# Value products over all 128 rows, conversions placed freely, reciprocal tile double and value tile single

## Chip, core and metric

The kernel runs on one NeuronCore of a Trainium2 chip, alone. The core has five engines that run side by side, each through its own list of instructions in a fixed order: TensorE (PE; its weight loads are shown apart, as PEld), VectorE (DVE), ScalarE (ACT), GpSimd (POOL) and SyncE (SP), whose list here is the queue that issues all transfers. The metric is the time on the device in microseconds; lower is better.

## What is computed

A block-causal attention over 4 batches, 8 heads, 576 positions and 64 channels is followed by two feed-forward layers, each with an inner width of 2048 over 2304 tokens of 512 channels. The weights of the layers come as 64-bit numbers.

```python
scores = scale * np.matmul(q, k.transpose(0, 1, 3, 2))
mask = block_i >= block_j                      # blocks of 64 positions
scores = np.where(mask, scores, -1000000000.0)
attn = np.exp(scores - np.max(scores, axis=-1, keepdims=True))
attn = attn / (np.sum(attn, axis=-1, keepdims=True) + 1e-09)
x = np.matmul(attn, v)                         # then (tokens, 512)
h = x @ w_in;  x = (h / (1 + np.exp(-h))) @ w_out
h = x @ w_in2; out = (h / (1 + np.exp(-1.702 * h))) @ w_out2
```

## The kernel before

**Pairs.** The attention works on 16 pairs of heads. Both heads of a pair fill the 128 rows. For each of nine blocks of 64 queries, `s_mm` forms the scores of both heads with a block-diagonal tile of the queries (`bd`) as the loaded operand and the keys as the streaming one. Every number is split into a rounded part and a residue (`qh`, `ql`, `kh`, `kl`, two halves of `va`, `pt0` and `pt1`), and three products take the place of one. `s_max` (L425, DVE) takes row maxima, `s_exp` (L435, ACT) exponentials with row sums, `t_mm` (L474, PE) transposes the probabilities in tiles of 128x128, `t_hi` (ACT, or DVE once) and `t_lo` (L492, DVE) split them into `pt0` and `pt1`.

**Value products.** `o_mm` multiplies values with transposed probabilities, head by head, in two halves of the query blocks. The loaded operand is 128 keys of the split values (`va`), the streaming one the probabilities of the query blocks that see these keys. The first half has four products (256 and 128 columns, for `pt0` and for `pt1`), the second half ten: 320, 320, 320, 192 and 64 columns, twice. 576 keys are four and a half tiles of 128, so the product of 64 columns has only 64 keys, and the kernel gives it 64 rows (L509). There are 32 blocks of ten, with 64 such products. The values are padded with zeros to 640 keys in memory (`layout_v`), and the last 64 columns of every probability tile of even index are set to zero once at the start (L595).

**Normalising.** `o_copy` moves the results to the tiles `e0` and `e1`, `x_shift` moves parts of them across the rows by transfers, and `x_add` adds (POOL). Reciprocals of the row sums (`r_inv`) go by way of a small tile and device memory (`r_mm`, `r_copy`, `r_put`) and come back spread over the rows as the tile `rb` (`r_get`, L465); `x_norm` (L545, POOL) multiplies. `rb` had one buffer. `v`, the value tile that `v_hi` (L326) and `v_lo` (L390) on POOL split into `va`, had two.

**Weights.** A weight piece of 128x512 arrives as 64-bit numbers in `raw` (two buffers, 512 KB, L232), and becomes single precision in six instructions: `w_scale` (L239, ACT), `w_bits` (L248, L250, DVE), `w_rest` (L260, L262, DVE) and `w_sum` (L270, POOL). Eight pieces are converted in the attention part; `w_part` enters one for every second pair, half of it in each of two rounds. The others follow in the feed-forward part.

**What sets the order.** Nothing is issued where it is written. `Flow.add` collects every operation with an assumed duration and what it reads and writes; `Flow.run` then plays them through: the engine that can start first takes, of its operations that are ready, the one with the lowest `at`. `at` comes from the table `plan`, whose rounds are 12.6 us (`TAU`) apart, pair after pair, in units of the planner's own clock. The argument `early` holds an operation back to a given planner time even when all it needs is there. `w_part` sets it to its own place plus 6 us (`T0`). The outcome is one fixed list per engine; on the chip an engine waits at each entry until its inputs and its buffer are free, and everything behind it on that engine waits too.

The feed-forward part has two layers in three phases each. A step forms one tile of the inner width (L667 to L669, 12 products), applies the activation (L682 to L687) and multiplies into four accumulators (L694 to L696, 12 products); the tokens go through in chunks of up to 512 (`xc`, L646 and L648).

Of the kernel before, what the change touches and what calls it, by code (L numbers as in the profile page):

```python
# [26 lines left out]
class Flow:  # L27
# [8 lines left out]
        self.wrote = {}  # L36
        self.read = {}

    def add(self, eng, us, fn, reads=(), writes=(), at=0.0, lag=0.0, size=0, after=(), name="", sb=False, early=0.0):
        op = Op()  # L40
        op.eng, op.us, op.fn, op.at, op.lag, op.size, op.name = eng, us, fn, at, lag, size, name
        op.outs, op.ready, op.end, op.idx, op.sb = [], early, 0.0, len(self.ops), sb
        deps = {id(x): x for x in after}
        for k in reads:
            w = self.wrote.get(k)
            if w is not None:
                deps[id(w)] = w
            self.read.setdefault(k, []).append(op)
        for k in writes:
            w = self.wrote.get(k)  # L50
            if w is not None:
                deps[id(w)] = w
            for x in self.read.get(k, ()):
                if x is not op:
                    deps[id(x)] = x
            self.wrote[k] = op
            self.read[k] = []
        op.left = len(deps)
        for x in deps.values():
            x.outs.append(op)  # L60
        self.ops.append(op)
        return op
# [47 lines left out]
def mm(n):  # L110
    return max(0.11, n / 2400 + 0.0135)
# [18 lines left out]
def block_causal_attention_two_ffn(  # L130
# [9 lines left out]
    nc = tc.nc  # L140
    PSUM = bass.MemoryType.PSUM

    NP, P, S = qT.shape
    BLK = 64
    NB = S // BLK
    NKT = vP.shape[2] // P
# [12 lines left out]
    NA = 4  # L159
    NWARM = 12  # L160
    TAU = 12.6
    T0 = 6.0
    LEAD = 12
    BEFORE = 1e4

    flow = Flow()
    add = flow.add
# [15 lines left out]
    def T(pool, shape, dt, name):  # L183
        if name not in tiles:
            tiles[name] = pools[pool].tile(shape, dt, tag=name, name=name)
        return tiles[name]

    bank = {i: T("psum", [P, 512], F32, f"bank{i}") for i in (0, 1, 4, 5, 6, 7)}
    sb = T("psum", [P, 2, 512], F32, "sb")
# [8 lines left out]
    def xkeys(m, c0, n):  # L198
        return [("xy", m, i) for i in range(c0 // H, (c0 + n - 1) // H + 1)]
# [25 lines left out]
    def w_load(op, n, i):  # L225
        l, f = divmod(n, NF)
        c = slice(i * DM, (i + 1) * DM)
        k = piece(n, i)
        if not WIDE:
            op("sp", 0.4, lambda: nc.sync.dma_start(out=wf_(k), in_=ws_[l][f][:, c]), (), [("wf", k % NWF)], size=P * DM * 4)  # L230
            return
        op("sp", 0.4, lambda: nc.sync.dma_start(  # L232
            out=raw_(k).rearrange("p d b -> p (d b)"), in_=ws_[l][f][:, c].bitcast(I32)), (), [("raw", k % 2)],
            size=P * DM * 8)
# [37 lines left out]
    def w_split(n, i, at):  # L272
        k = piece(n, i)
        kw, kh, kl = ("wf", k % NWF), ("ws", n % NS, i, 0), ("ws", n % NS, i, 1)
        add("act", 0.53, lambda: nc.scalar.copy(slot(n, i)[:, 0, :], wf_(k)), [kw], [kh], at, after=slot_after(n))  # L275
        add("pool", 1.28, lambda: nc.gpsimd.tensor_sub(slot(n, i)[:, 1, :], wf_(k), f32(slot(n, i)[:, 0, :])),  # L276
            [kw, kh], [kl], at, after=slot_after(n))
# [9 lines left out]

    ends = {"a1": [], "a2": [], "a3": []}
    clock = [0.0]
    early = [0.0]  # L290

    def op(eng, us, fn, reads=(), writes=(), lag=0.0, size=0, sb=False):
        x = add(eng, us, fn, reads, writes, clock[0] - BEFORE, lag=lag, size=size, name="att", sb=sb, early=early[0])
        for y in ends:
            ends[y].append(x)
        return x
# [13 lines left out]
    def a1(p, n):  # L310
        return T("a1", [P, S], F32 if n in "qk" else F32R, n + (str(p % 2) if n in ("kh", "kl") else ""))

    def ka1(p, n):
        return (n, p % 2 if n in ("kh", "kl") else 0)

    def a3(p, n, shape=None, dt=F32):
        return T("a3", shape or [P, S], dt, f"{n}_{p % 2}")

    def pt(p, i):
        return T("a2" if p % 2 == 0 else "a3", [P, nat, P], F32R, f"pt{i}_{p % 2}")  # L320
# [14 lines left out]
    def take(what, key):  # L335
        if what == "s":
            held[key] = S_BANK[key[2]]
        else:
            turn[what] += 1
            held[key] = ring[what][turn[what] % len(ring[what])]  # L340
        return held[key]

    def src(p, n):
        if p == 0 and n in "qk":
            return a3(0, {"q": "e0", "k": "e1"}[n]), ("e", 0, "qk".index(n))
        if n == "v":
            return a3(p, "v", [P, NKT * 2 * BLK]), ("v", p % 2)
        return a1(p, n), ka1(p, n)

    def load(p, n):  # L350
        t, k = src(p, n)
        d = {"q": qT, "k": kT, "v": vP}[n]
        op("sp", 0.4, lambda: nc.sync.dma_start(out=t, in_=d[p]), (), [k], size=P * d.shape[2] * 4)

    def q_hi(p, eng):
        (q, k), t = src(p, "q"), a1(p, "qh")
        op("act", act(S), lambda: nc.scalar.mul(t, q, BLK ** -0.5), [k], [ka1(p, "qh")])
# [4 lines left out]
    def q_lo(p):  # L362
        (q, k), t, hi = src(p, "q"), a1(p, "ql"), a1(p, "qh")
        op("dve", 0.67, lambda: q_sub(t, q, hi), [k, ka1(p, "qh")], [ka1(p, "ql")], sb=True)
# [16 lines left out]
    def va_(p):  # L381
        return a3(p, "va", [P, NKT * 2, 2, BLK], F32R)
# [71 lines left out]
    def rd_(p):  # L454
        return T("drp", [2, NB, BLK], F32, f"rd{p % 2}")
# [3 lines left out]
        op("sp", 0.4, lambda: nc.sync.dma_start(out=rd_(p).rearrange("h j q -> j h q"), in_=rt), [("rt", 0)], [("rd", p % 2)])  # L459

    def r_get(p):
        rb = a3(0, "rb")
        for h, r in enumerate((A, B)):
            s = rd_(p)[h:h + 1].rearrange("h j q -> h (j q)").to_broadcast([BLK, S])
            op("sp", 0.65, lambda r=r, s=s: nc.sync.dma_start(out=rb[r], in_=s), [("rd", p % 2)], [("rb", 0, h)],  # L465
               size=P * S * 2)

    def t_mm(p, g):
# [26 lines left out]
    def o_mm(p, h, half):  # L495
        j0, j1 = halves[half]
        n = (j1 - j0) * BLK
        b = take("o", ("o", p, h, half))
        o = bank[b]
        va = va_(p)  # L500
        seq = [(i, kt) for i in (0, 1) for kt in range(NKT) if 2 * kt < j1]
        fs = {fidx[kt, j] for _, kt in seq for j in range(max(j0, 2 * kt), j1)}
        gs = [g for g, x in enumerate(groups) if fs & set(x)]

        def mms():
            for a, (i, kt) in enumerate(seq):
                js = max(j0, 2 * kt)
                f = fidx[kt, js]
                r = slice(0, P if 2 * kt + 1 < NB else BLK)  # L509
                w = va[r, 2 * kt + h, :, :].rearrange("p a b -> p (a b)")  # L510
                x = pt(p, i)[r, f:f + j1 - js, h * BLK:(h + 1) * BLK]
                nc.tensor.matmul(o[:, (js - j0) * BLK:n], w, x, start=(a == 0), stop=(a == len(seq) - 1))  # L512

        us = sum(mm((j1 - max(j0, 2 * kt)) * BLK) * 1.05 for i, kt in seq)
        op("pe", us, mms, [("pt", p % 2, g, i) for g in gs for i in range(2)] + [("va", p % 2, 0), ("va", p % 2, 1)], [("B", b)], lag=0.2)
# [25 lines left out]

    def x_norm(p):
        b, hp = divmod(p, PPB)
        x, rb = a3(p, "x"), a3(0, "rb")
        op("pool", 1.45, lambda: nc.gpsimd.tensor_mul(xy[:, hp, b * S:(b + 1) * S], x, rb),  # L545
           [("x", p % 2, 0), ("x", p % 2, 1), ("rb", 0, 0), ("rb", 0, 1)], xkeys(hp, b * S, S))

    def w_part(p, stage):
        n = divmod((p + 1) // 2, 2)
        if p < 1 or n[0] >= NA or (stage < 2) != (p % 2 == 1):  # L550
            return
        early[0] = clock[0] + T0
        (w_scale, w_bits, w_rest, w_sum)[stage](op, *n)
        if stage == 2 and n != (NA - 1, 1):
            w_load(op, n[0] + n[1], 1 - n[1])
        early[0] = 0.0

    plan = [
        (0, s_mm, 3), (1, s_exp, 4), (0, s_max, 3), (2, o_mm, 0, 0), (1, t_mm, 2), (1, t_hi, 0, "act"),
# [10 lines left out]
        (0, s_exp, 5), (0, s_mm, 1), (1, t_mm, 5), (1, v_lo, "pool"), (1, t_mm, 1), (1, r_put),  # L570
        (0, w_part, 3), (0, s_max, 1), (0, s_mm, 4), (1, t_hi, 5, "dve"), (2, o_copy, 1, 1, "act"),
        (1, t_lo, 5), (0, s_exp, 1), (1, t_hi, 1, "act"), (2, r_get), (0, s_max, 4), (0, t_mm, 0),
        (1, t_lo, 1),
    ]
# [230 lines left out]
```

## Time and profile before

| | us |
|---|---|
| median of three runs | 1046.88 (1041.76 to 1050.94) |
| the profiled execution, its own time | 1043.87 |
| its span from the first to the last instruction | 1041.8 |
| PE busy | 1007.7 (97%) |
| DVE busy | 698.9 (67%) |
| ACT busy | 485.4 (47%) |
| POOL busy | 326.4 (31%) |

A busy share is the time in which an engine had an instruction in progress. Matmuls are pipelined: the next one starts before the one before it ends, and a busy TensorE is not one at its peak. How far matmuls really follow each other is read from the distance between their starts. The page's chain of work goes back from the last instruction, at each step to what released it; 80% of it is PE and 13% DVE. The idle time in a row is that of its engine just before the instruction, with what ended it.

### The profile page before, as it was taken

The page shows a single profiled execution, that of the slowest core. Times are in us where ns is not written, and L with a number is a line of the kernel's source. Part 1 is how long each engine was busy: PE and PEld are TensorE (multiplying, and loading weights), DVE is VectorE, ACT ScalarE, POOL GpSimd, SP SyncE. Part 2 cuts the span into 40 slices and gives each one's busy share as a digit, 9 for nine tenths or more (in the row PEclk, how much of TensorE's full clock was granted, in tenths as well). Part 3 has the DMA queues.
Part 4 walks back from the last instruction along what each step waited for, and adds up shares of the span by engine and source line. Part 5 has one row for each costly group of instructions (what it writes and reads, how often), then busy time and mean ns, then how long its engine had stood idle before and what let it go on. Part 6 is the DMA issues. An engine that isn't in the chain of part 4 may idle for free.

```text
span 1041.8 us, 14408 instructions
## 1 busy us (share of the span) xinstructions
PE 1007.7 (97%) x5196; PEld 854.1 (82%) x5196; DVE 698.9 (67%) x1144; ACT 485.4 (47%) x1055; POOL 326.4 (31%) x238
## 2 busy tenths in 40 slices
PE   7899999988999999999999999999999999999998
PEld 5788878776888898888988888888888888888887
DVE  6689987778989769954798348962359444454333
ACT  5677777675545355432543235442345332343221
POOL 6557665658544245210342006310016000000000
PEclk8999999999999999999999999999999999999999
DMA  6777867733234413542244111321112222112222
GB/s 180 177 182 169 207 162 178 192 84 93 72 117 156 137 66 127 176 142 81 81 142 133 50 41 57 106 102 41 41 54 89 81 81 81 62 61 81 81 82 81
DMA packets 84616, 112.67 MB, mean 108 GB/s; under 512 B 41920, under 2 KB 46528, under 8 KB 84544
## 3 DMA queue, kind: packets, MB, share of 16 engines
q1 hardware_dynamic: 84544, 111.74, 35.9%
q8 instruction: 41, 0.67, 0.3%
q14 instruction: 31, 0.25, 0.1%
HBM read 72.12 MB, written 23.67 MB: 92 GB/s over the span
## 4 chain that ended last, share of the span: by engine, by line
PE 80%; DVE 13%; ACT 3%; issue 2%; DMA 1%; POOL 0%; DVEq 0%; SPq 0%; ACTq 0%; POOLq 0%
PE bank L668 11%; PE bank L667 11%; PE bank L669 11%; PE sb L694 6%; PE sb L696 6%; PE sb L695 6%; PE bank L694 6%; PE bank L696 6%; PE bank L695 6%; PE bank L512 5%; PE bank L474 4%; DVE xc L648 2%; DVE mx L425 1%; DVE wf L250 1%; DVE pt L492 1%
## 5 line engine op out<-in xcount | busy, mean ns | idle before, releaser
L684 DVE SCALAR_TENSOR_TENSOR th<-th,bank 128x512 f32<-128x512 f32 (+1 forms) x160 | 100.9, 630 | 211.3 <-ACT th L682 211.0
L667 PE MATMUL bank<-xc,ws 128*128 128x512 f32 (+1 forms) x640 | 236.0, 369 | 0.0
L668 PE MATMUL bank<-xc,ws 128*128 128x512 f32 (+1 forms) x640 | 235.9, 369 | 0.0
L669 PE MATMUL bank<-xc,ws 128*128 128x512 f32 (+1 forms) x640 | 235.7, 368 | 0.0
L682 ACT ACTIVATE th<-bank 128x512 f32<-128x512 f32 (+1 forms) x160 | 88.6, 554 | 301.8 <-PE bank L669 295.9
L276 POOL TENSOR_TENSOR ws<-wf,ws 128x512 fp32r<-128x512 f32 x64 | 93.9, 1481 | 237.2 <-ACT ws L275 237.2
L686 ACT CAST g<-th 128x512 fp32r<-128x512 f32 (+1 forms) x160 | 92.5, 578 | 118.4 <-DVE th L684 118.3
L687 DVE TENSOR_TENSOR g<-th,g 128x512 fp32r<-128x512 f32 (+1 forms) x160 | 111.6, 698 | 45.3 <-ACT g L686 44.3
L270 POOL TENSOR_TENSOR wf<-wf,wt 128x512 f32<-128x512 f32 x64 | 91.2, 1425 | 160.4 <-DVE wt L262 160.4
L669 PEld LDWEIGHTS bank<-xc,ws 128*128 128x128 f32 x640 | 120.7, 189 | 20.4 <-DVE xc L648 0.2
L667 PEld LDWEIGHTS bank<-xc,ws 128*128 128x128 f32 x640 | 120.7, 189 | 20.1
L668 PEld LDWEIGHTS bank<-xc,ws 128*128 128x128 f32 x640 | 120.7, 189 | 19.8
L694 PE MATMUL sb<-g,ws 128*128 128x512 f32 (+1 forms) x320 | 118.4, 370 | 4.4 <-ACT g L686 2.6
L696 PE MATMUL sb<-g,ws 128*128 128x512 f32 (+1 forms) x320 | 118.0, 369 | 0.4 <-DVE g L687 0.4
L694 PE MATMUL bank<-g,ws 128*128 128x512 f32 (+1 forms) x320 | 117.9, 369 | 0.0
L695 PE MATMUL bank<-g,ws 128*128 128x512 f32 (+1 forms) x320 | 117.9, 368 | 0.0
L695 PE MATMUL sb<-g,ws 128*128 128x512 f32 (+1 forms) x320 | 117.9, 368 | 0.0
L696 PE MATMUL bank<-g,ws 128*128 128x512 f32 (+1 forms) x320 | 117.8, 368 | 0.0
L648 DVE TENSOR_TENSOR xc<-xy,xc 128x512 fp32r<-128x512 f32 (+1 forms) x120 | 93.6, 798 | 17.5 <-PE bank L668 10.7
L512 PE MATMUL bank<-pt,va 128*128 128x320 f32 (+3 forms) x448 | 84.2, 309 | 1.8 <-DVE e L327 1.3
L492 DVE TENSOR_TENSOR pt<-bank,pt 128x512 fp32r<-128x512 f32 (+1 forms) x112 | 68.7, 624 | 18.2 <-ACT pt L324 17.6
L512 PEld LDWEIGHTS bank<-pt,va 128*128 128x128 f32 (+1 forms) x448 | 69.3, 194 | 13.5 <-DVE e L327 2.3
(76 smaller groups left out, 1617.2 us busy)
## 6 DMA issues: line engine op xcount, KB each, us to landing
raw<-w SPq DMA_DIRECT2D x64, 512.0 KB
yd<-yst SPq DMA_DIRECT2D x64, 256.0 KB
yst<-yd SPq DMA_DIRECT2D x64, 256.0 KB
v<-vP SPq DMA_DIRECT2D x16, 320.0 KB
k<-kT SPq DMA_DIRECT2D x16, 288.0 KB
rb<-rd SPq DMA_DIRECT2D x32, 144.0 KB
x<-e SPq DMA_DIRECT2D x32, 144.0 KB
q<-qT SPq DMA_DIRECT2D x15, 288.0 KB
```

What stands on the lines that cost most here:

```text
L276: add("pool", 1.28, lambda: nc.gpsimd.tensor_sub(slot(n, i)[:, 1, :], wf_(k), f32(slot(n, i)[:, 0, :])), [kw, kh], [kl], at, after=slot_af ...
L512: nc.tensor.matmul(o[:, (js - j0) * BLK:n], w, x, start=(a == 0), stop=(a == len(seq) - 1))
L648: add("dve", dve(n) + 0.01, lambda view=view, s=s: nc.vector.tensor_sub(view(1), s, f32(view(0))), xkeys(kt, c0, n) + [Kh], [Kl], tx, afte ...
L667: nc.tensor.matmul(h, w[:, 0, c], view(0), start=kt == 0, stop=False)
L668: nc.tensor.matmul(h, w[:, 1, c], view(0), start=False, stop=False)
L669: nc.tensor.matmul(h, w[:, 0, c], view(1), start=False, stop=kt == ND - 1)
L684: add("dve", dve(n), lambda th=th, h=h: nc.vector.scalar_tensor_tensor(out=th(), in0=th(), scalar=1.0, in1=h, op0=ALU.add, op1=ALU.mult), ...
L686: add("act", act(n) + 0.05, lambda th=th, g=g: nc.scalar.copy(g(0), th()), [kth], [kgh], t, after=e2)
L687: add("dve", dve(n) + 0.01, lambda th=th, g=g: nc.vector.tensor_sub(g(1), th(), f32(g(0))), [kth, kgh], [kgl], t, after=e2, sb=True)
L694: nc.tensor.matmul(y, w[:, 0, c], g(0), start=st, stop=False)
L695: nc.tensor.matmul(y, w[:, 1, c], g(0), start=False, stop=False)
L696: nc.tensor.matmul(y, w[:, 0, c], g(1), start=False, stop=sp)
```

## The change

The value product of the last key tile takes all 128 rows of `va` and of `pt`. `early` and `T0` are gone, so that a conversion stands wherever the planner finds its engine free and its data there. `rb` has two buffers, one for each parity of the pair; `v` has one for all pairs. With these the order of nearly all instructions of the attention part changes.

```diff
-    def add(self, eng, us, fn, reads=(), writes=(), at=0.0, lag=0.0, size=0, after=(), name="", sb=False, early=0.0):
+    def add(self, eng, us, fn, reads=(), writes=(), at=0.0, lag=0.0, size=0, after=(), name="", sb=False):
...
-        op.outs, op.ready, op.end, op.idx, op.sb = [], early, 0.0, len(self.ops), sb
+        op.outs, op.ready, op.end, op.idx, op.sb = [], 0.0, 0.0, len(self.ops), sb
...
-            return a3(p, "v", [P, NKT * 2 * BLK]), ("v", p % 2)
+            return a3(0, "v", [P, NKT * 2 * BLK]), ("v", 0)
...
     def r_get(p):
-        rb = a3(0, "rb")
+        rb = a3(p, "rb")
...
-            op("sp", 0.65, lambda r=r, s=s: nc.sync.dma_start(out=rb[r], in_=s), [("rd", p % 2)], [("rb", 0, h)],
+            op("sp", 0.65, lambda r=r, s=s: nc.sync.dma_start(out=rb[r], in_=s), [("rd", p % 2)], [("rb", p % 2, h)],
...
-                r = slice(0, P if 2 * kt + 1 < NB else BLK)
-                w = va[r, 2 * kt + h, :, :].rearrange("p a b -> p (a b)")
-                x = pt(p, i)[r, f:f + j1 - js, h * BLK:(h + 1) * BLK]
+                w = va[:, 2 * kt + h, :, :].rearrange("p a b -> p (a b)")
+                x = pt(p, i)[:, f:f + j1 - js, h * BLK:(h + 1) * BLK]
...
-        x, rb = a3(p, "x"), a3(0, "rb")
+        x, rb = a3(p, "x"), a3(p, "rb")
...
-           [("x", p % 2, 0), ("x", p % 2, 1), ("rb", 0, 0), ("rb", 0, 1)], xkeys(hp, b * S, S))
+           [("x", p % 2, 0), ("x", p % 2, 1), ("rb", p % 2, 0), ("rb", p % 2, 1)], xkeys(hp, b * S, S))
...
-        early[0] = clock[0] + T0
         (w_scale, w_bits, w_rest, w_sum)[stage](op, *n)
         if stage == 2 and n != (NA - 1, 1):
             w_load(op, n[0] + n[1], 1 - n[1])
-        early[0] = 0.0
```

Lines of the changed kernel are one to three lower than those of the kernel before: the four DVE steps of a conversion are L247, L249, L259 and L261 there. DVE before, in the first pair, from the end of the first piece's conversion (`wt` is the work tile of a piece, `mx` a row maximum, `pt_0_115` a residue of transposed probabilities):

```order
L262 SCALAR_TENSOR_TENSOR wt_102<-raw_108,wt_102 128x512
L492 TENSOR_TENSOR pt_0_115<-bank_74,pt_0_111 128x512
L425 TENSOR_REDUCE mx_0_275<-bank_73 128x1
L441 TENSOR_SCALAR r_114<-l_96 128x9
L442 RECIPROCAL r_114<-r_114 128x9
L492 TENSOR_TENSOR pt_0_115<-bank_75,pt_0_111 128x512
L492 TENSOR_TENSOR pt_0_115<-bank_74,pt_0_111 128x512
L492 TENSOR_TENSOR pt_0_115<-bank_75,pt_0_111 128x512
L327 COPY e_0_84<-bank_77 128x256
```

The same place with the change:

```order
L261 SCALAR_TENSOR_TENSOR wt_102<-raw_108,wt_102 128x512
L247 TENSOR_SCALAR wt_121<-wf_120 128x512
L249 SCALAR_TENSOR_TENSOR wf_120<-wf_120,wt_121 128x512
L423 TENSOR_REDUCE mx_0_276<-bank_73 128x1
L490 TENSOR_TENSOR pt_0_115<-bank_74,pt_0_111 128x512
L259 TENSOR_SCALAR wt_121<-wf_120 128x512
L439 TENSOR_SCALAR r_114<-l_96 128x9
L261 SCALAR_TENSOR_TENSOR wt_121<-raw_133,wt_121 128x512
L440 RECIPROCAL r_114<-r_114 128x9
L490 TENSOR_TENSOR pt_0_115<-bank_75,pt_0_111 128x512
```

The second piece follows the first at once. All eight stand within DVE's first 165 rows, where the last ended at row 337 before; 17 of their 32 instructions stand ahead of the widest row maximum of the fourth pair (10 before), all 32 ahead of that of the tenth (20 before).

PE before, from the first pair's second block of four value products on (`bank_77` and `bank_76` take value products, `p` are probabilities, `bd_91` and `kh_99` belong to the second pair):

```order
L512 MATMUL bank_77<-pt_0_115,va_118 128x128
L474 MATMUL bank_75<-ident,p_8_105 128x128
L512 MATMUL bank_76<-pt_0_111,va_118 128x320 x3
L512 MATMUL bank_76<-pt_0_111,va_118 128x192
L512 MATMUL bank_76<-pt_0_111,va_118 128x64
L512 MATMUL bank_76<-pt_0_115,va_118 128x320 x3
L512 MATMUL bank_76<-pt_0_115,va_118 128x192
L512 MATMUL bank_76<-pt_0_115,va_118 128x64
L412 MATMUL sb<-kh_99,bd_91 128x256
L413 MATMUL sb<-kl_104,bd_91 128x256
L414 MATMUL sb<-kh_99,bd_92 128x256
```

With the change, from the first pair's first block of four on:

```order
L509 MATMUL bank_77<-pt_0_115,va_118 128x128
L410 MATMUL sb<-kh_99,bd_91 128x256
L411 MATMUL sb<-kl_104,bd_91 128x256
L412 MATMUL sb<-kh_99,bd_92 128x256
L410 MATMUL bank_73<-kh_99,bd_91 128x512
L411 MATMUL bank_73<-kl_104,bd_91 128x512
L412 MATMUL bank_73<-kh_99,bd_92 128x512
L410 MATMUL bank_72<-kh_99,bd_91 128x64
L411 MATMUL bank_72<-kl_104,bd_91 128x64
L412 MATMUL bank_72<-kh_99,bd_92 128x64
L472 MATMUL bank_75<-ident,p_5_107 128x128
```

The second pair's scores moved ahead of the first pair's remaining transposes and of its blocks of ten. The queue (SP) before, in a round of the middle part (`v` are value loads, `bd` the block queries of a later pair, `rb` reciprocals, `x` and `e` shifts of results):

```order
L353 DMA k<-kT 128x576
L535 DMA x_139<-e_1_141 64x576
L465 DMA rb_136<-rd_142 64x576 x2
L535 DMA e_1_138<-e_1_141 64x576
L353 DMA v_132<-vP 128x640
L370 DMA bd_91<-qh 64x9x64 x2
```

A round with the change:

```order
L351 DMA k<-kT 128x576
L351 DMA v_117<-vP 128x640
L532 DMA e_0_84<-e_0_85 64x576
L463 DMA rb_141<-rd_142 64x576
L368 DMA bd_89<-qh 64x9x64 x2
L368 DMA bd_90<-ql 64x9x64 x2
```

The value load stands ahead of the shift and of the reciprocals now, always fills `v_117`, and still stands ahead of the block queries.

## Rows read from the trace of the kernel before

**Rows 1.** Busy time by stretch, all engines; us from the start, busy us (instructions), granted clock.

```profile
core 0: us, PE busy (x) PEld busy (x) DVE busy (x) ACT busy (x) POOL busy (x), PEclk, DMA share, GB/s
0.00:59.00 59.00, 47.44 (x244) 39.14 (x245) 38.39 (x85) 35.26 (x95) 31.62 (x35) 0.88 0.71 176
59.00:137.00 78.00, 73.06 (x489) 63.10 (x488) 72.06 (x135) 59.75 (x173) 54.23 (x38) 1.00 0.75 184
137.00:223.00 86.00, 78.39 (x512) 68.17 (x511) 69.20 (x139) 61.60 (x178) 53.58 (x38) 0.98 0.65 168
223.00:254.00 31.00, 26.97 (x155) 22.12 (x153) 26.04 (x36) 20.18 (x46) 24.31 (x17) 1.00 0.26 69
254.00:1042.00 788.00, 781.83 (x3802) 661.58 (x3802) 493.18 (x753) 308.64 (x563) 162.68 (x112) 1.00 0.27 91
```

**Rows 2.** The same for DVE's instructions on the conversions' work tile (`wt`) alone.

```profile
0.00:59.00 59.00, 6.06 (x10) 0.88 0.71 176
59.00:137.00 78.00, 10.62 (x10) 1.00 0.75 184
137.00:223.00 86.00, 7.88 (x12) 0.98 0.65 168
```

**Rows 3.** Value products by form: count, busy us, mean ns, idle us before them.

```profile
L512 PEld LDWEIGHTS bank<-pt,va 128*128 128x128 f32 x384 | 57.4, 195 | 4.7 <-DVE e L327 2.3 <-DVE pt L327 0.8
...
L512 PEld LDWEIGHTS bank<-pt,va 64*128 64x128 f32 x64 | 11.9, 186 | 8.7 <-issue 0.4
```

**Rows 4.** TensorE in order of time: start us, duration us, line, out<-in, rows*columns loaded, streamed.

```profile
109.81 0.31 PE L413 MATMUL sb<-kl,bd 128*128 128x320 f32 x1
109.95 0.31 PE L414 MATMUL sb<-kh,bd 128*128 128x320 f32 x1
...
124.24 0.28 PE L414 MATMUL bank<-kh,bd 128*128 128x192 f32 x1
124.35 1.89 PE L512 MATMUL bank<-pt,va 128*128 128x320 f32 x10
126.17 0.66 PE L474 MATMUL bank<-ident,p 128*128 128x128 f32 x4
```

**Rows 5.** Chain that ended last, in order of time: start us, us, what.

```profile
26.30 2.33 PE bank L512 x8
...
208.27 0.77 DVE wt L260
...
209.22 1.62 DVE wt L262
...
233.04 1.71 PE bank L512 x10
```

**Rows 6.** The start in order of time: GpSimd's key split, TensorE's first scores after it.

```profile
22.08 1.42 POOL L379 TENSOR_TENSOR kl<-k,kh 128x576 fp32r<-128x576 f32 x1
...
28.56 0.58 PE L412 MATMUL sb<-kh,bd 128*128 128x256 f32 x1
```

**Rows 7.** Queue, value split, transfer on the chain, score product; waits between 59 and 223 us.

```profile
110.72 1.29 SPq L370 DMA_DIRECT2D bd<-ql  x2
...
112.05 1.26 POOL L326 TENSOR_TENSOR va<-v,one 128x640 fp32r<-128x640 f32 x1 [2.00 <-PE bank L512]
...
114.59 3.09 DMA e<-e
...
115.08 1.56 POOL L390 TENSOR_TENSOR va<-v,va 128x640 fp32r<-128x640 f32 x1
...
116.67 0.52 SPq L353 DMA_DIRECT2D v<-vP  x1
...
117.16 0.28 PE L414 MATMUL sb<-kh,bd 128*128 128x256 f32 x1
...
POOL va L326 <- PE bank L512: 24.7, 8, 6.4
...
SPq L465 <- POOL xy L545: 8.7, 7, 2.9
```

More of the change, by code (lines that the diff above doesn't have):

```diff
@@ L161, in block_causal_attention_two_ffn @@
     TAU = 12.6
-    T0 = 6.0
     LEAD = 12
@@ L289, in block_causal_attention_two_ffn @@
     clock = [0.0]
-    early = [0.0]
     def op(eng, us, fn, reads=(), writes=(), lag=0.0, size=0, sb=False):
-        x = add(eng, us, fn, reads, writes, clock[0] - BEFORE, lag=lag, size=size, name="att", sb=sb, early=early[0])
+        x = add(eng, us, fn, reads, writes, clock[0] - BEFORE, lag=lag, size=size, name="att", sb=sb)
         for y in ends:
```

## Prediction

> **What bounds the kernel now.** I read the busy times by stretch first [rows 1]. From 254 us to the end TensorE is busy for 781.83 of 788 us: the feed-forward part waits for nothing but its own products, and the change's new order of work has run out by then. So only the first 254 us can move. There TensorE is busy for 47.44 of 59 us at a granted clock of 0.88, then 73.06 of 78, 78.39 of 86 and 26.97 of 31 us. VectorE (DVE) is its close second: 72.06 of 78 us between 59 and 137 us, which leaves it 5.9 us, but 69.20 of 86 us afterwards, and only 38.39 of 59 us at the start, which leaves it 20.6 us. What is saved on TensorE counts in full only where DVE has room.
>
> Next the value products (L512) by form [rows 3]. The 64 weight loads over 64 rows take 186 ns against 195 ns for the 384 over 128 rows, but the load path stands idle for 8.7 us ahead of them, 136 ns each, against 4.7 us, 12 ns each, ahead of the full ones. The busy share of TensorE hides this: each matmul before such a load is drawn as busy. The distances between starts show it [rows 4]. Full-row matmuls of 320 columns follow each other at 0.14 us (109.81 to 109.95), those of 192 columns at 0.11 us (124.24 to 124.35); the ten value products of the second half of one head take 1.82 us (124.35 to 126.17).
>
> Last the chain that ended last [rows 5]: between the first and the last row shown, 24 of the 32 blocks of ten lie on it (4 before 59 us, 6 up to 137, 11 up to 223, 3 after; the one at 26.30 is cut to its eight last products). Between them it runs through DVE and ScalarE, and at 208.27 and 209.22 us through a weight conversion: L260 and L262 hold the row maxima behind them for 0.77 and 1.62 us.
>
> **The products over 128 rows.** The operands are there already: the values are zero-padded in memory, and the last columns of the even probability tiles are cleared, so the 64 added rows add zeros. The instruction count stays. If all ten products keep the full-row pace, a block has six of 320 columns at 0.14, and four of 192 and 64 columns at no more than 0.11: 0.84 + 0.44 = 1.28 us against 1.82, a gain of 0.54. I take 0.5. The 24 blocks on the chain give 12 us, all 32 give 16 us, and a stall that has another cause than the row count gives 0.
>
> The Trainium skill speaks on both sides here. Its page "TensorE: Matmul & The Clock Gate" (section "LDWEIGHTS (loading the stationary operand)") says that a load's time goes by its columns and that fewer rows do not change it. The page "TensorEngine Tiling (Array Packing)", section "Key Properties", says that a change of tiling mode drains the engine. By the first alone the edit is worth nothing, by the second about what the distances give. The trace agrees with the first on the load itself (186 and 195 ns) and with the second on the wait ahead of it (136 and 12 ns).
>
> **The conversions.** Each of the eight weight pieces costs four DVE instructions in the attention part. They are no longer held to 6 us after their place in the plan, and the order places all eight within the first 165 rows of DVE, where before the eighth ended at row 337. Two and a half ran before 59 us, two and a half up to 137, three up to 223 us [rows 2]. At 59 and 137 us the widest row maximum of the fourth and of the tenth pair was running; in the new order 17 of the 32 instructions stand ahead of the first of these, and the other 15 between the two: 4.25 and 3.75 pieces. A piece cost 6.06/2.5 = 2.4 us at the start, 10.62/2.5 = 4.2 in the middle, and 7.88/3 = 2.6 later.
>
> At the start 1.75 more pieces are 4.2 us in DVE's 20.6 us of idle time; I count 0, and if they stand ahead of waiting maxima up to 4.2. In the middle 1.25 more pieces are 5.3 us against 5.9 us of room, which the shorter TensorE stretch wants too; I count +4, between 0 and 5.3. Later 7.9 us of DVE work is gone, 2.4 us of it seen on the chain, and with it the TensorE idle time behind it; I count -3, between 0 and -7.9. ScalarE's, GpSimd's and the queue's parts of each piece (one scaling, one sum, one load of 512 KB) move with it and beside them.
>
> **The start.** The scores of the second pair now stand ahead of the first pair's last products in TensorE's order, and its key split ahead of a second value split on GpSimd. Before, that key split ended at 22.08 + 1.42 = 23.50 us and the scores began at 28.56 [rows 6]: at most 5.1 us, at least 0. The clock was down for part of this stretch, and the pieces added there pull the other way. I count -1, near the lower bound, since the work passed over must still be done.
>
> **The buffers.** The reciprocal row has two buffers, so its load need not wait for the product that reads the old one: 8.7 us of the queue's waits between 59 and 223 us [rows 7]. The block queries behind it landed before the scores wanted them, so I count 0; 8.7 us is the far bound. The value tile has one buffer: its load now waits for the split of the pair just before instead of two before. The row shows such a wait already: a split ends at 115.08 + 1.56 = 116.64 us and the load leaves at 116.67 [rows 7]. The value split itself runs more than a round after its load, so 0 again; the cost if the queue behind is held is a rival below.
>
> **The sum.** The profiled execution took 1043.9 us (span 1041.8), 3.0 under the median of 1046.9. Start: 4 x 0.5 = -2 and -1. Middle: 6 x 0.5 = -3 and +4. Later: 11 x 0.5 = -5.5 and -3. Tail: 3 x 0.5 = -1.5. Feed-forward: 0. Together -12: **1032 us**.
>
> **Rivals.**
> - *DVE takes it back.* DVE has 5.9 us of room in the middle; if the moved pieces cost 5.3 there and 4.2 at the start, nothing of the products' gain survives in the middle, and the later relief meets no chain, the sum is -2 + 4.2 + 5.3 - 5.5 - 1.5 = +0.5: 1044 us. For it: 92% busy there [rows 1]. Against it: at the start DVE mostly waits.
> - *All of it counts.* All 32 blocks (-16), the start's -5.1 and half of the later conversions' bound (-4): 1019 us. For it: with conversions gone DVE has over 24 us free between 137 and 223 us. Against it: eight blocks were off the chain.
> - *The rows are not the cause.* The waits stay, only the order moves: -1 + 4 - 3 = 0, 1044 us. This is what the skill's rule on loads would give. Against it: every one of the 64 loads has the wait, and full loads between them do not.
> - *Slower: one value buffer holds the queue.* The queue works in order. The value load stands a few rows ahead of the next pair's block queries and now waits for a split that itself waits for TensorE (24.7 us in eight waits, 3.1 each, 6.4 at most). The block queries of the residue (ql) left at 110.72, took 1.29 to issue and, by a transfer of the same size, 3.09 to land: 115.1 us, and the score product that reads them began at 117.16 [rows 7]. So 2.1 us late is free. A wait of 3.1 with the two halves of a split behind it (1.26 and 1.56) is 5.9 us: 3.8 beyond, over some 13 pairs 49 us: 1081. From 3.0 us late per pair the gain is gone, from 4.1 the kernel is slower by over 1%. Against it: the load's place in the queue moved back along with its wait.
>
> **How the numbers follow.** The forecast has 0.52 with its own range 1027 to 1037, "DVE takes it back" 0.18, "all of it counts" 0.12, "the rows are not the cause" 0.08, the held queue 0.10. The likeliest gives 1032. With the queue's rival and half of the best case left out, 0.16 in all, the range is 1020 to 1045 us. A measurement of this kernel can tell about 1%: faster is under 1036.4, slower over 1057.3. Faster takes 0.48 of the forecast and the 0.12: 0.60. Slower has 0.08 of the queue's 0.10. The same has the rest: 0.04 + 0.18 + 0.08 + 0.02 = 0.32.
>
> **What would show it.** The form of 64 rows is gone, ten products take about 1.3 us, and the idle time ahead of their loads falls from 13.4 to about 5 us. DVE's conversions stand before 137 us, and the chain after it holds none. The first down product starts some 12 us before its old place, and the stretch after it still takes 788 us. The forecast is wrong if blocks stay at 1.8 us (the rows), if DVE is over 95% busy from 59 to 137 us and that stretch grows (the conversions), or if TensorE waits for scores behind late block queries (the queue).

## The result and the profile after

The changed kernel takes 1031.3 us (median of six, 1029.4 to 1035.7), the kernel before 1045.9 in the same comparison: a ratio of 0.986 (0.982 to 0.990). The forecast was 1032. The profiled execution is the longest of the six, 1035.7 us with a span of 1033.9, so its trace shows less of the gain than the median does.

The stretches below end, like those of [rows 1], at the widest row maximum of the fourth, the tenth and the last pair and shortly after the first down product. Columns as in [rows 1].

```profile
0.00:53.80 53.80, 41.80 (x233) 34.71 (x234) 46.23 (x91) 34.15 (x93) 33.76 (x35) 0.90 0.82 198
53.80:141.50 87.70, 78.01 (x515) 69.91 (x514) 72.71 (x143) 63.29 (x181) 60.83 (x44) 0.92 0.76 185
141.50:215.40 73.90, 65.47 (x480) 60.58 (x480) 59.87 (x124) 56.48 (x167) 46.61 (x33) 1.00 0.67 168
215.40:246.00 30.60, 27.79 (x173) 23.07 (x173) 25.50 (x38) 21.95 (x52) 20.72 (x14) 1.00 0.27 65
246.00:1034.00 788.00, 781.73 (x3802) 660.88 (x3800) 497.53 (x753) 308.68 (x563) 166.49 (x114) 1.00 0.27 91
```

The start is 5.2 us shorter than before, the middle 9.7 us longer, the stretch after it 12.1 us shorter, and the rest unchanged. The middle, forecast as nearly unchanged, is where this kernel loses. Its granted clock is 0.92 where it had been 1.00. DVE is busy for 83% of it, not for over 95%; the narrower stretches further below show where DVE is full.

The value products by form (as [rows 3]) and one block of ten in TensorE's order of time (as [rows 4]):

```profile
L509 PEld LDWEIGHTS bank<-pt,va 128*128 128x128 f32 x448 | 65.5, 197 | 6.8 <-DVE e L325 5.4 <-DVE pt L490 0.5
```

```profile
100.86 1.42 PE L509 MATMUL bank<-pt,va 128*128 128x320 f32 x10
102.12 0.66 PE L472 MATMUL bank<-ident,p 128*128 128x128 f32 x4
```

The ten products take 1.26 us from start to start (102.12 - 100.86), before 1.82, and the load path's idle time ahead of all 448 loads is 6.8 us, before 13.4.

DVE's conversions alone (as [rows 2]), and the longest of their rows on the chain of waits behind 40 us. Seven rows stand on it between 39 and 62 us, 4.1 us together; behind the last row shown the chain meets no conversion until 237 us, in the feed-forward part:

```profile
0.00:53.80 53.80, 13.95 (x17) 0.90 0.82 198
53.80:141.50 87.70, 14.45 (x15) 0.92 0.76 185
141.50:215.40 73.90, 0.00 (x0) 1.00 0.67 168
```

```profile
41.60 1.04 DVE wt L259
...
71.41 1.70 DVE wt L261
...
87.04 1.59 DVE wt L261
...
91.95 1.35 DVE wf L249
```

The places are those forecast: 17 of 32 instructions in the start, 15 in the middle. DVE spends 28.4 us on them, somewhat more than the forecast's 6.06 + 10.62 [rows 2] and 4.2 + 5.3 added, 26.2.

The first scores of the second pair, and the first down product (the first that multiplies an activated tile into the accumulators), in TensorE's order of time; the third row is the down product in the kernel before:

```profile
24.15 0.52 PE L410 MATMUL sb<-kh,bd 128*128 128x256 f32 x1
```

```profile
244.90 0.50 PE L689 MATMUL sb<-g,ws 128*128 128x512 f32 x1 [1.41 <-ACT g L681]
```

```profile
253.08 0.50 PE L694 MATMUL sb<-g,ws 128*128 128x512 f32 x1 [2.64 <-ACT g L686]
```

Those scores had begun at 28.56 us [rows 6]. The down product comes 8.2 us earlier in these two executions, of which the one before was 2 to 3 us under its median and the changed one 4.4 over.

### The profile page after: what moved, and what is told of

Same layout as the page of the kernel before. It is cut to its first block, busy times and chain, and to the rows that moved or that the text cites. A ratio compares the mean times of both kernels' runs of the same rounds, so it can differ in the third digit from the quotient of the medians.

```text
span 1033.9 us, 14401 instructions
## 1 busy us (share of the span) xinstructions
PE 994.8 (96%) x5196; PEld 849.1 (82%) x5196; DVE 701.8 (68%) x1144; ACT 484.5 (47%) x1055; POOL 328.4 (32%) x238
## 4 chain that ended last, share of the span: by engine, by line
PE 73%; DVE 17%; ACT 4%; issue 3%; DMA 1%; POOL 1%; SPq 0%; DVEq 0%; ACTq 0%; POOLq 0%
PE bank L663 11%; PE bank L664 11%; PE bank L662 11%; PE sb L689 6%; PE sb L690 6%; PE sb L691 6%; PE bank L690 6%; PE bank L689 6%; PE bank L691 6%; DVE pt L490 3%; DVE mx L423 3%; PE bank L509 2%; PE bank L472 2%; DVE wf L249 2%; DVE xc L643 1%
## 5 line engine op out<-in xcount | busy, mean ns | idle before, releaser
L682 DVE TENSOR_TENSOR g<-th,g 128x512 fp32r<-128x512 f32 (+1 forms) x160 | 114.9, 718 | 47.5 <-ACT g L681 46.3
L643 DVE TENSOR_TENSOR xc<-xy,xc 128x512 fp32r<-128x512 f32 (+1 forms) x120 | 90.0, 766 | 17.8 <-PE bank L663 10.7
L472 PE MATMUL bank<-ident,p 128*128 128x128 f32 x400 | 66.2, 291 | 14.2 <-DVE pt L490 10.5
L641 ACT CAST xc<-xy 128x512 fp32r<-128x512 f32 (+1 forms) x120 | 67.3, 577 | 26.0 <-PE bank L663 24.5
```

The lines of the kernel that those rows point to most:

```text
L643: add("dve", dve(n) + 0.01, lambda view=view, s=s: nc.vector.tensor_sub(view(1), s, f32(view(0))), xkeys(kt, c0, n) + [Kh], [Kl], tx, afte ...
L682: add("dve", dve(n) + 0.01, lambda th=th, g=g: nc.vector.tensor_sub(g(1), th(), f32(g(0))), [kth, kgh], [kgl], t, after=e2, sb=True)
```

## The parts one by one

Two readings were at hand: the products bring nearly all of it, as forecast; or the new order of all the other instructions has a large share, of either sign. Four kernels did one part alone or undid one.

**The rows alone.** Nothing else moves: the planner's costs are the same, and the order on every engine too.

```diff
-                r = slice(0, P if 2 * kt + 1 < NB else BLK)
-                w = va[r, 2 * kt + h, :, :].rearrange("p a b -> p (a b)")
+                w = va[:, 2 * kt + h, :, :].rearrange("p a b -> p (a b)")
```

> The kernel before with the value products over 128 rows alone; the order of every engine stays as before. Theory 1 (the products bring nearly all of it): a block of ten falls from 1.87 to about 1.25 us; 24 of 32 blocks on the chain give 15 us, a ratio of 0.986. Rival (the new order brings half): the products give 6 to 8 us, 0.993. Rival (the new order costs something, since DVE is filled at the start and TensorE's clock falls twice in the middle): the products alone give nearly all 32 x 0.62 = 20 us, 0.981, and this kernel is faster than the changed one.

1039.7 us against 1047.1, ratio 0.992 (0.990 to 0.995): 7.4 us of the 12 forecast. Its stretches between the same maxima as in [rows 1]:

```profile
58.00:136.00 78.00, 68.06 (x490) 61.20 (x488) 72.77 (x135) 58.97 (x173) 54.19 (x38) 1.00 0.76 184
136.00:218.60 82.60, 72.71 (x513) 65.80 (x511) 72.07 (x140) 60.60 (x178) 54.69 (x38) 0.98 0.69 175
```

In the middle TensorE is busy for 68.06 us where it was 73.06, and the stretch is 78.0 us long as before: the 5 us turned into idle time. DVE, in the same order, works for 72.77 us there. This is the rival "DVE takes it back", in one stretch. TensorE's transposes wait 5.4 us there for DVE's residue steps, 2.5 before; ScalarE's exponentials wait 11.1 us for row maxima, 7.5 before. Behind it, where DVE had more room, the stretch is 3.4 us shorter. The two profiled executions differ by 4.0 us in all, so the stretches show a part of the 7.4.

**The new order with 64 rows,** the changed kernel with the rows taken back:

```diff
-                w = va[:, 2 * kt + h, :, :].rearrange("p a b -> p (a b)")
+                r = slice(0, P if 2 * kt + 1 < NB else BLK)
+                w = va[r, 2 * kt + h, :, :].rearrange("p a b -> p (a b)")
```

> The changed kernel with its value products back on 64 rows in the last key block; its new order stays. Theory 1 (the products bring nearly all): as the kernel before, ratio 0.998 to 1.003. Rival (the new order brings half): 0.993. Rival (the new order costs some 5 us, which the products hide): 1.005.

1041.6 us, 0.9945 (0.992 to 0.997). So the order without the rows is worth 5.5 us, and the rows on top of it 10.3 by the medians, 8.9 by the two ratios, which come from separate comparisons.

**The conversions alone, and the buffers alone:**

```diff
-        early[0] = clock[0] + T0
+        early[0] = 0.0
```

> The kernel before with the conversions no longer held to their place, alone (64 rows and buffers as before). Theory 1: +4 in the middle, -3 later, so 0 to +1 us, ratio 1.000. Rival (released conversions take DVE off the chain later): -4 us, 0.996. Rival (filling DVE at the start costs): +5 us, 1.005, with a start and a middle stretch in which DVE is over 90% busy and TensorE idle more than before.

```diff
-            return a3(p, "v", [P, NKT * 2 * BLK]), ("v", p % 2)
+            return a3(0, "v", [P, NKT * 2 * BLK]), ("v", 0)
...
-        rb = a3(0, "rb")
+        rb = a3(p, "rb")
```

> The kernel before with the buffers alone: two reciprocal rows, one value tile (two reciprocal rows alone find no room). Theory 1: 0, ratio 0.998 to 1.002. Rival (the queue's 8.7 us of waits for the reciprocal row counted): up to -4 us, 0.996. Rival (the single value tile holds the queue): +5 us or more, 1.005, with value loads that leave right at the end of a value split and block queries behind them that land after TensorE wants them.

The conversions alone: 1047.2 us, 1.000 (0.999 to 1.002). The buffers alone, costed at nothing: 1032.9 us, 0.987 (0.985 to 0.990), as much as the whole change. The parts do not add up: -7.4, 0 and -14 would make -21, and the change brought -14.6. Two questions follow: what in the buffers brings 14 us, and what takes 7 us back.

## Buffers or order

**One value tile alone:**

```diff
-            return a3(p, "v", [P, NKT * 2 * BLK]), ("v", p % 2)
+            return a3(0, "v", [P, NKT * 2 * BLK]), ("v", 0)
```

> The kernel before with one value tile alone; one reciprocal row as before, 64 rows as before. The planner makes another order for it. Theory 1 (the second reciprocal row brings the buffers' 13 us, by the 8.7 us of the queue's waits and what hangs on them): a single value tile can only add waits, ratio 1.000 to 1.005. Theory 2 (the buffers' gain comes from the order that the planner makes around the single value tile): 0.987 already here. Theory 3 (half from each): 0.993.

1034.7 us, 0.988 (0.985 to 0.990): nearly all of the buffers' gain, from a change that only takes room away. The other 1.8 us come with the second reciprocal row, for which the planner makes yet another order; the two intervals overlap almost wholly and do not tell it from nothing.

**The same order with two value tiles in memory.** The planner is told of one tile, the tiles stay two:

```diff
-            return a3(p, "v", [P, NKT * 2 * BLK]), ("v", p % 2)
+            return a3(p, "v", [P, NKT * 2 * BLK]), ("v", 0)
```

> The order that the planner makes for a single value tile, but with two value tiles in memory as before: what differs from the kernel before is the order alone, and what differs from the run with one value tile is the wait for it alone. If the 12 us come from the order: ratio 0.985 to 0.990, as with one tile. If they came from the single tile itself, 1.000.

1035.7 us, 0.989 (0.986 to 0.991): the same. The gain is the order's. The wait of the single tile is real and costs nothing that these runs can tell; in the run with one tile the queue waits ten times for the split, by the waits between 59 and 223 us, and the run with two has no such wait:

```profile
SPq L353 <- POOL va L390: 12.7, 10, 1.9
```

**Another order for no reason.** One figure of the planner's arithmetic, and nothing that the chip executes:

```diff
-    SEM = 0.06
+    SEM = 0.07
```

> The kernel before with one figure of the planner's arithmetic changed, 0.07 us for a semaphore instead of 0.06: the same instructions, tiles and buffers in another order. Theory 1 (any reshuffling of the order moves the time by some 10 us either way, and the gain of the buffer changes is such an accident): off by over 3 us, anywhere from 0.985 to 1.01. Theory 2 (the order around the single value tile is better for a reason, and the order before is a usual one): 0.998 to 1.002.

1035.9 us, 0.990 (0.988 to 0.992). A figure without any meaning for the chip brings 11.5 us. So the gain need not be a merit of the buffers; the order of the kernel before is worse than three other orders of the same work, which lie between 1032.9 and 1035.9 us. Its stretches:

```profile
0.00:53.20 53.20, 42.66 (x232) 34.94 (x233) 39.03 (x82) 34.04 (x93) 31.25 (x34) 0.94 0.71 182
53.20:131.30 78.10, 73.20 (x499) 64.41 (x498) 65.82 (x138) 60.34 (x173) 51.82 (x37) 1.00 0.76 191
131.30:214.80 83.50, 76.36 (x508) 67.88 (x507) 70.54 (x139) 61.05 (x178) 56.05 (x39) 0.98 0.72 172
```

The start is 5.8 us shorter than in [rows 1] at a clock of 0.94 instead of 0.88, the middle equal, the third stretch 2.5 us shorter. The first scores of the second pair stand at 25.26 us (first row below), although GpSimd does the same splits in the same order up to that point as before: before, they had waited behind TensorE's own list, where the eight value products of [rows 5] run until 28.56, and not behind the key split.

```profile
25.26 0.35 PE L412 MATMUL sb<-kh,bd 128*128 128x256 f32 x1
```

A part of the 11.5 us goes with TensorE's clock. The mean granted clock of the kernel before was 0.984 to 0.993 in its runs, here 0.993 to 0.995. At 0.993 the kernel before took 1041.8 to 1042.8 us in three runs, and this one 1037.0 in its only one: by my estimate from these the order is worth some 5 to 6 us at a like clock. Whether a lower clock made the waits or the waits the lower clock, these runs do not show.

## What takes it back

**Rows and buffers, without the release of the conversions:**

```diff
-                r = slice(0, P if 2 * kt + 1 < NB else BLK)
...
-            return a3(p, "v", [P, NKT * 2 * BLK]), ("v", p % 2)
+            return a3(0, "v", [P, NKT * 2 * BLK]), ("v", 0)
...
-        rb = a3(0, "rb")
+        rb = a3(p, "rb")
```

> The value products over 128 rows and both buffer changes, without the release of the conversions: the order is that of the buffers alone. Theory 1 (the products give the 7 to 10 us seen in the other two orders here too): 1023 to 1025 us, ratio 0.978 to 0.980, faster than the changed kernel. Rival (products and buffers remove the same waiting, and VectorE is the limit behind both): 1031, 0.986. Rival (TensorE is the bound in this order, busy for all of 60 to 74 us, so the products' whole 16 us count): 1017, 0.972.

1021.8 us, 0.976 (0.974 to 0.979): faster than both kernels, and 9.5 us faster than the whole change. The release of the conversions costs that much here. With the planner's other figure, once without and once with the release:

> Products over 128 rows and both buffer changes, no release of the conversions, with the planner's figure of 0.07: another order for the fastest kernel so far (0.976). Theory 2: 0.974 to 0.979 again. Theory 1: anywhere from 0.968 to 0.995.

> The whole change with the planner's figure of 0.07. If the release of the conversions costs for a reason (VectorE filled at the start), it is slower than the run with products and buffers and the same figure by about 9 us, as without the new figure. If the 9 us were an accident of the order, the difference is of any size or sign.

1021.4 us, 0.976 (0.974 to 0.978), without the release, and 1026.5, 0.981 (0.979 to 0.983), with it. And at 64 rows the buffers' order loses 8.7 us by it (1032.9 to 1041.6). So the release costs 9.5 us at 128 rows and 8.7 at 64 in the order of the buffers, which is the same for both, and 5.1 in the order with the other figure, where about 9 were expected. In the order before it costs nothing.

Where, the stretch from 38 to 68 us shows: all engines, then DVE's conversions from 0 to 38 and from 38 to 68 us. First rows and buffers without the release:

```profile
38.00:68.00 30.00, 26.62 (x199) 24.22 (x198) 27.90 (x56) 25.35 (x72) 21.65 (x17) 1.00 0.83 212
```

```profile
0.00:38.00 38.00, 4.75 (x6) 0.96 0.78 183
38.00:68.00 30.00, 5.41 (x6) 1.00 0.83 212
```

Then the changed kernel:

```profile
38.00:68.00 30.00, 26.51 (x181) 22.54 (x180) 29.94 (x58) 21.73 (x67) 21.19 (x15) 1.00 0.98 218
```

```profile
0.00:38.00 38.00, 10.55 (x13) 0.87 0.75 187
38.00:68.00 30.00, 8.82 (x9) 1.00 0.98 218
```

DVE is busy for 29.94 of 30 us; 19.4 us of its first 68 are conversions, against 10.2. TensorE starts 18 matmuls fewer in this stretch. A stretch that begins 6 us before the end of this one in the changed kernel, and the one after that:

```profile
62.00:75.00 13.00, 9.76 (x66) 8.10 (x65) 12.91 (x24) 9.38 (x28) 8.27 (x7) 0.98 0.87 220
75.00:82.00 7.00, 7.00 (x32) 6.76 (x33) 4.42 (x11) 2.91 (x8) 4.98 (x4) 0.54 0.41 133
```

TensorE stands idle for a quarter of 13 us, most of it for DVE, which hardly rests, and then its granted clock is 0.54 over 7 us, which is 1.2 GHz, the lower of its two levels, for nearly all of them; from 92 to 99 us once more. The kernel with rows and buffers alone has 1.00 from 38 to 68 us and two such drops of half that length, from 108 and from 187 us on. The lower clock is not what the release costs: at a mean granted clock of 0.995 the changed kernel took 1030.5 and 1030.8 us, and rows and buffers alone took 1021.2 to 1024.2 in three runs. The widest maximum of the sixth pair comes at 85.8 us, in rows and buffers alone at 71.6: 14.2 us later. With most conversions done by then, 3.1 us come back by the last pair (215.4 against 204.3). The sixth pair's maximum in the changed kernel, then the sixth and the last pair's in rows and buffers alone:

```profile
85.76 0.75 DVE L423 TENSOR_REDUCE mx<-sb 128x1 f32<-128x576 f32 x1
```

```profile
71.59 0.75 DVE L425 TENSOR_REDUCE mx<-sb 128x1 f32<-128x576 f32 x1
...
204.30 0.75 DVE L425 TENSOR_REDUCE mx<-sb 128x1 f32<-128x576 f32 x1
```

The two other pairs of kernels have the same shape: the changed kernel's order at 64 rows is 12.9 us behind the buffers alone at that maximum and 8.6 at the last, and with the other figure it is 5.8 and 2.7.

In the order before the release brings the same delay, and it is the return that hides it: the sixth pair's maximum comes at 89.4 us with the release alone and at 78.6 without it, 10.8 us later, and the last pair's at 225.6 and 223.3.

```profile
89.41 0.76 DVE L425 TENSOR_REDUCE mx<-sb 128x1 f32<-128x576 f32 x1 [0.84 <-PE sb L414]
```

```profile
78.61 0.76 DVE L425 TENSOR_REDUCE mx<-sb 128x1 f32<-128x576 f32 x1 [0.62 <-PE sb L414]
```

Here 8.5 us come back, not 3 to 4. In the kernel before, the chain behind its sixth pair runs through DVE's conversions for 6.1 us, the three rows below and the two of [rows 5]; with the release it meets none there. In rows and buffers alone such rows make 3.6 us. That this is what comes back fits in size, but is argued: the release moves other entries of the lists too.

```profile
82.40 1.32 DVE wt L248
83.75 1.80 DVE wf L250
...
99.11 0.63 DVE wt L262
```

## What stalls at 64 rows

The block of ten fell as forecast, but that does not say whether a product over 64 rows costs, or the change between 128 and 64. Two kernels with more of them tell it.

```diff
-                r = slice(0, P if 2 * kt + 1 < NB else BLK)
+                r = slice(0, P if kt < 3 else BLK)
```

> The kernel before with the products of key blocks 7 and 8 (the last two of each five) over 64 rows, so that the 64-row products stand in pairs side by side; half of key block 7 is left out of the sum. If each change between 128 and 64 rows costs, a block of ten stays at about 1.87 us and the time at 1.000. If each 64-row product costs 0.31 us ((1.87 - 1.25)/2), a block takes 2.5 us and the kernel up to 20 us more (1.015 to 1.02).

```diff
-                r = slice(0, P if 2 * kt + 1 < NB else BLK)
+                r = slice(0, P if kt not in (1, 4) else BLK)
```

> The kernel before with the products of the second key tile over 64 rows as well, away from the last ones; half of that tile is left out of the sum. A block of ten then changes the row count eight times instead of four (the change to the last one's neighbours counted), and a block of four, four times instead of none. If each change costs, or each 64-row product does, a block of ten takes 2.5 us, a block of four 0.6 us more than before, and the kernel up to 128 x 0.31 = 40 us more (1.02 to 1.04). If only the short product of 64 columns stalls, the blocks keep their times, ratio 1.000.

Side by side: 1049.6 us, 1.003 (1.001 to 1.005). Apart: 1099.6, 1.050 (1.047 to 1.054). The loads over 64 rows, first side by side, then apart (as [rows 3]), and blocks of ten, of ten and of four in order of time:

```profile
L512 PEld LDWEIGHTS bank<-pt,va 64*128 64x128 f32 x128 | 19.3, 188 | 12.5 <-issue 12.5
```

```profile
126.18 1.93 PE L512 MATMUL bank<-pt,va 128*128 128x320 f32 x10
128.04 0.66 PE L474 MATMUL bank<-ident,p 128*128 128x128 f32 x4
```

```profile
L512 PEld LDWEIGHTS bank<-pt,va 64*128 64x128 f32 x192 | 39.2, 204 | 31.9 <-issue 18.9 <-ACT e L324 0.3
```

```profile
144.29 2.66 PE L512 MATMUL bank<-pt,va 128*128 128x320 f32 x10
146.88 0.66 PE L474 MATMUL bank<-ident,p 128*128 128x128 f32 x4
...
147.81 1.10 PE L512 MATMUL bank<-pt,va 128*128 128x256 f32 x4
148.84 0.44 PE L412 MATMUL bank<-kh,bd 128*128 128x384 f32 x1
```

Twice as many 64-row products side by side leave the block at 1.86 us; eight changes instead of four make it 2.59, and a block of four with four changes takes 1.03. Over the blocks that ran at full clock and without idle time (23 to 30 of each kernel's 32 blocks of ten, 18 and 25 of those of four) the medians for ten are 1.31, 1.87, 1.92 and 2.65 us (no change, four, four with twice the products, eight), for four 0.49 and 1.11. A change costs 0.14 to 0.2 us, at 320 columns too; a 64-row product behind another costs nothing. The rule "Mode switching requires drain" of the Trainium skill, page "TensorEngine Tiling (Array Packing)", section "Key Properties", fits this, if a change of the row count is taken for such a switch; the page gives no price.

The run with the products apart takes 52.8 us more than the kernel before, where at most 40 were expected. Its blocks account for some 45 (32 times 0.78 and 32 times 0.62); the rest is not taken apart, and its granted clock was lower, as shown at the end.

## Why the forecast was right, step by step

**The products: the block right, what it is worth right only in some orders.** 1.28 us was forecast for ten products, 1.26 measured, and the stall goes with the row count's changes, as the place of the idle time had said. "24 blocks on the chain give 12 us" came to 7.4 us in the order before, 10.3 in the changed one, 11.1 in the buffers' order. The step that failed in the first is the chain as a measure: a block on the chain counts only as far as the next engine has room, and in the middle DVE had 5.9 us on paper and gave none. The 12 us were a fair figure for the better order.

**The conversions: the place right, the price wrong.** "At the start 1.75 more pieces are 4.2 us in DVE's 20.6 us of idle time; I count 0" and "Later ... I count -3" are the steps that failed: the net was +1 in the sum and is +5 to +9.5 in the two other orders; in the order before it is 0, as forecast, by a delay of 10.8 us and a return of 8.5 in the profiled executions. DVE's idle time at the start was not room. It came between steps that pass back and forth between TensorE, ScalarE and DVE, and a conversion that the planner puts ahead of a row maximum makes the steps behind it late: seven conversion rows stand on the changed kernel's chain between 39 and 62 us. Both upper bounds given, 4.2 and 5.3, together come near what was measured. The rival "DVE takes it back" was the right mechanism for this part; it had to be joined to the forecast, not set against it. The reading of the chain also passed over 3.75 us of conversions in the middle, at 82.40, 83.75 and 99.11 us, so no relief was counted there.

**The start: the wrong end of the range.** "At most 5.1 us, at least 0 ... I count -1": it was 4.4 (28.56 to 24.15), on TensorE's own list.

**What the sum had no term for** is the order as a whole. It treated the order before as neutral and priced only the instructions named. The other orders show it to be 11 to 14 us worse than what the planner makes after each of the three nudges tried (one value tile, both buffers, another figure). With the other figure the profiled executions differ by 8.5 us, of which the start and the third stretch hold 8.3; how much of it is the lower clock, and which entries of the lists do the rest beyond the scores of the second pair, stays open. How wide further nudges would spread was not tried.

**The buffers: right.** The reciprocal row's waits were off the path (1.8 us go with them, within the intervals), and the value tile's 12.7 us cost nothing: the rival of the held queue has fallen.

**The feed-forward part: right,** 789.0 us from the first down product against 788.7.

So the time was right by luck: two terms of some 10 us were missing with opposite signs, the better order and the released conversions. A smaller piece of luck is the base: the sum took its 12 us from the profiled execution, 1043.9; from the median of 1046.9 it would have been 1034.9. Step by step along the runs it reads -14.2 (the buffers' order), -11.1 (the rows), +9.5 (the release), together -15.8, against -14.6 measured at once; medians of separate comparisons differ by about that much.

## To carry along

Where a scheduler writes the order, change one number that means nothing and time it before crediting an edit: here that alone moved the time by 11.5 us, four fifths of what the edit did. Undo the parts of a change one by one on top of each other, for a part that shows nothing alone (the release of the conversions) may cost 9 us in a better order; the kernel without it takes 1021.8 us. Idle time of an engine that alternates with others on a chain is not room for more work.

## What the runs showed of the hardware

**More changes of the row count, a lower clock.** In the run with eight changes in a block of ten, in the same order of work as before, TensorE is drawn busy for 275.71 of the first 292 us, and yet its granted clock there is 0.87, where the kernel before has 0.88 for its start alone and 0.98 to 1.00 from 59 us on [rows 1]:

```profile
0.00:292.00 292.00, 275.71 (x1338) 211.42 (x1339) 190.36 (x382) 173.17 (x482) 148.54 (x119) 0.87 0.55 139
```

Fewer changes did not raise it: with none (the rows alone) it is 0.88 to 58 us and 0.98 from there to 290 us. Nor did more 64-row products at four changes lower it: 0.88 to 59 us and 0.99 from there to 292. What it is in eight changes that lowers the clock, the runs do not show.

**A DVE instruction waits inside its own duration.** The scaling of nine columns (`r<-l`) takes 0.16 us or anything up to 1.5. In the changed kernel, DVE and GpSimd in order of time:

```profile
187.83 0.77 DVE L439 TENSOR_SCALAR r<-l 128x9 f32<-128x9 f32 x1
```

```profile
186.77 1.80 POOL L377 TENSOR_TENSOR kl<-k,kh 128x576 fp32r<-128x576 f32 x1
```

```profile
201.89 0.16 DVE L439 TENSOR_SCALAR r<-l 128x9 f32<-128x9 f32 x1
```

The first ends at 188.60, just after GpSimd's split at 188.57; during the second GpSimd does nothing. The Trainium skill has this in "SBUF — State Buffer", section "Who interferes with whom": the two share a port pair, and where an instruction of DVE takes it, whoever comes second waits for the other's whole instruction. So a busy DVE here is partly a waiting one, and a conversion costs by what runs on GpSimd beside it: in the kernel before, its second step took 0.68 us at 26.70 us, with GpSimd idle, and 1.80 at 83.75, with GpSimd busy all along, and a piece took 2.4 to 4.2 us [rows 2].
